# Four lines instead of five for VectorE's exponentials, with one of them on GpSimd: a gated attention kernel on one core

## The chip, the cores and the metric

The kernel runs on one core of one Trainium2 chip. The metric is the device time of one execution in microseconds. The core has TensorE (PE in the profile, its weight loads PEld), VectorE (DVE), ScalarE (ACT), GpSimd (POOL) and SyncE (SP, which here issues DMAs).

## What is computed

One input of 2048 tokens by 512 features goes through two attention branches, which are mixed by a gate. Cut to what matters:

```python
H, Dh = 32, 16                                   # both branches: 32 heads of 16
# branch A: softmax attention over all 2048 keys
q, k, v = split(x @ A_wqkv)
p = softmax(einsum("bhqd,bhkd->bhqk", q, k) * Dh ** -0.5)
a = einsum("bhqk,bhkd->bhqd", p, v) @ A_wo
# branch B: linear attention with feature maps
phi = lambda t: concat(softmax(t @ w_phi), softmax(-(t @ w_phi)))
kv, z = einsum(phi(k), v), phi(k).sum(tokens)
b = (phi(q) @ kv / (phi(q) @ z + 1e-6)) @ B_wo
g = sigmoid((x * gate_w).sum(-1, keepdims=True))
out = g * a + (1 - g) * b
```

Weights, input and output are bf16. Branch A has 32 x 2048 x 2048 = 134 million exponentials, and these fill the time.

## The kernel before

**Tiles.** A unit is one tile of scores: 128 keys by 512 queries of one head. A pack is four units, of four heads. There are 4 chunks of queries, 8 groups of four heads and 16 blocks of keys, so 512 packs and 2048 units. The scores of up to four heads are computed beside each other in the rows of TensorE's array (`_scores`), into PSUM. The exponentials of a pack are multiplied with the values of its four heads beside each other in the columns (`_values`), and add up in one PSUM bank; a column of ones in the values gives the softmax's denominator. So an approximate exponential needs no maximum, and a factor that all of a row's terms share would cancel.

**Two ways to an exponential.** Most units go to ScalarE: `_exp` takes groups of three and two units from a ring of five PSUM banks (`NRING`, `GROUPS`), and writes bf16 into `ET`. The packs that `SHARES` names (so many of the 16 packs of each group of heads) go to VectorE in `_vector_batch`. There four instructions named `v_bits` move the four score tiles from PSUM to a block of 128x2048 fp16, scaled. Then five instructions named `v_line` each add a constant of `LINES` to the block, cut it off at zero and write the result as int16 into another block: the bits, read as bf16, are a piecewise linear exponential. The five differ by a shift, and their sum is closer to the exponential than one is. TensorE multiplies each of the five with the values (`pvx`), so that the sum is made in PSUM. The blocks are a ring of `NBLK` buffers; the last line of a pack overwrites its input block.

**Other work of VectorE.** It evicts all projections from PSUM, normalizes branch A (`_normed`: `n_t1`, `n_den`, `n_rec`, `n_mul`, `n_back`) and makes the softmax of branch B's feature maps (`_b_part`, the names with `b_`). GpSimd fills constants at the start and does nothing after that. TensorE also runs products with a zero operand (`_fill`) that add nothing to the result.

**Order.** Nothing is ordered by loops. Each operation is given to a planner (`Plan.op`) with a cost, a priority and what it reads and writes. `Plan.order` simulates the engines with these costs and fixes one order of instructions for each engine, `Plan._waits` derives the semaphores from the dependencies, and `emit` writes the program. The tables `HURRY`, `EASE`, `QEASE`, `LEASE`, `OEASE` and `NUDGE` shift priorities of single operations. Each engine runs its list in order, so an instruction that waits holds up all that is behind it on its engine.

Of the kernel before, what the change touches and what calls it, by code (L numbers as in the profile page):

```python
# [7 lines left out]
ALU = mybir.AluOpType  # L8
AX = mybir.AxisListType

P = 128
# [9 lines left out]
LINES = (15902.272, 15921.612, 15944.747, 15969.563, 16002.022)  # L21
# [22 lines left out]
class Op:  # L44
    def __init__(self, eng, fn, cost, name, prio, rel, kind, lat, groups=None):
# [6 lines left out]
        self.need = False  # L52
        self.acquire = None
# [15 lines left out]
class Plan:  # L69
# [11 lines left out]
    LATE = 9.5  # L81

# [73 lines left out]
    def order(self):  # L156
# [9 lines left out]
        pe = (None, (0.0,) * 4, 0.0)  # L166
        recent = []
# [5 lines left out]
        while left:  # L173
            best = None
            for e in self.ENGS:
                found, limit = [], 1e9
                for o in avail[e]:
# [83 lines left out]
            else:  # L261
# [3 lines left out]
                free[e] = o.end  # L265
            queues[e].append(o)
            left -= 1
# [103 lines left out]
class _Kernel:  # L371
# [5 lines left out]
    NBLK, LEAD = 7, 4  # L377
# [7 lines left out]
    OREL = 5  # L385
    ENDS = 10
    HURRY = (2.9, 1.9, -1.8, 7.6, -1.0, -4.5, 21.3, 1.1, 0.8, 0.0, 8.8, 2.1, 8.3, -5.2, 0.0, 0.0, 1.3, -3.6, 0.0, 0.0, 0.0,
# [4 lines left out]
    QEASE = (0, 0.0, 13.2, 0.0, 5.2, -10.0, 15.5, 0.2, 0.0, 5.8, -9.4, -3.4, 2.9, 7.9, 0.0, 3.2)  # L392
    LEASE = (0.4, 3.6, -6.9, 0.7, -0.7, -0.7, -13.7, 20.2, -4.9, 11.4)
    OEASE = (14.9, 0.6, -1.3, 18.1, 9.6, 11.8, 25, 9.7, 0.8, -5.2, 1.0, 3.6, 6.4, 0, 0, 0)
    EASE = (0.0, 1.2, 0.4, 8.9, 0.0, 0.0, 2.6, 0.0, 0.0, -3.6, 11.9, 0.0, 3.7, 1.9, -4.9, -1.5, 11.8, 2.3, 2.1, 0.0, 0.3, -0.9,
# [4 lines left out]
    NUDGE = {  # L400
        'b_even': {10: 1.3},
        'b_grid': {7: 15.3, 8: 16.2},
        'b_max': {1: -22.3, 3: 17.1, 13: 1.8, 18: -26.3, 20: -8.7, 22: -4.2, 24: 8.3, 31: 2.8, 37: 25.7, 50: -15.5,
            52: -17.0, 57: -15.0, 58: -4.1, 59: -17.8, 60: 8.7, 61: 3.5, 75: 18.1},
        'b_mul': {7: -11.9},
        'b_octave': {1: 2.1, 2: 5.8},
        'b_out': {14: 13.9},
        'b_part': {1: 12.9},
        'b_slope': {8: -4.1},
        'b_square': {3: -9.2, 4: 3.0, 10: -10.4},  # L410
        'b_sum': {20: -16.6},
        'b_top': {4: 5.4, 18: 11.1},
        'bv': {1: 3.4, 5: 7.0, 7: -2.3, 8: 23.3, 13: -5.3, 14: -18.8, 28: 7.4, 29: -3.5, 42: 7.7},
        'den': {20: 18.4, 26: 10.5},
        'kproj': {1: -5.8, 13: -7.7, 21: 5.1, 24: 5.0, 29: 9.7, 33: 4.1, 36: -11.3, 45: 10.9, 53: -3.2, 61: 4.4, 64: 14.2},
        'kproj_ev': {11: -6.1},
        'n_back': {3: 5.6, 14: -6.3},
        'n_den': {4: -7.0, 11: 10.1, 18: -4.3},
        'n_rec': {9: 30.0},
        'n_t1': {7: 5.1, 11: -15.8, 18: 3.7, 21: -10.4},  # L420
        'num': {6: 16.9},
        'out_ev': {4: -7.4, 11: -21.6},
        'outa': {14: -2.6, 22: -6.7, 27: -11.9, 35: -14.0, 36: 4.1, 37: 6.8, 56: 1.4, 57: -11.0},
        'pq': {6: 18.3, 13: -4.0, 20: 7.4, 25: -11.0, 33: 30.0, 42: 26.3, 53: -4.4, 57: -6.4, 61: 6.2, 65: -2.7, 81: 2.9,
            85: 2.4, 87: 9.1, 95: 6.2, 113: -12.4, 115: -7.9, 117: -12.5, 128: 11.3},
        'pq_ev': {16: 5.7},
        'pvx': {4: 12.2, 6: 5.5, 7: 24.2, 9: -2.8, 10: -10.3, 14: -16.0, 16: -24.7, 17: -6.4, 18: -3.2, 19: 1.7, 33: -3.7,
# [3 lines left out]
        'qproj_ev': {11: -19.0, 14: -6.7, 18: 9.1, 19: -2.2},  # L431
        'v_bits': {58: 19.2, 215: 15.2},
        'v_line': {1: 20.1, 4: 6.9, 9: -10.7, 28: 14.5, 30: -9.2, 32: 9.9, 33: 16.5, 40: -13.6, 44: 7.7, 68: -9.4, 71: -16.6,
# [7 lines left out]
        'vproj': {23: 23.6, 26: 4.1, 28: 9.2, 41: 3.1, 49: 3.9, 51: -7.7, 60: 18.9, 61: 3.2},  # L441
        'vqk': {4: 11.2, 6: -19.7, 9: 15.9, 14: 10.3, 19: 8.4, 22: 13.9, 26: -23.0, 28: -5.9, 33: -28.9, 35: -2.8, 46: -14.6,
# [36 lines left out]
    def _memory(self, ctx):  # L479
# [1153 lines left out]
```

## Time and profile before

| | |
|---|---|
| median of 3 runs | 788.67 us (788.64 to 789.07) |
| the profiled execution's time | 788.6 us |
| its span in the trace | 786.6 us |
| granted TensorE clock | 1.0 |
| exponentials on ScalarE | 683 instructions for 1708 units |
| packs on VectorE | 85, with 340 `v_bits` and 425 `v_line` |
| instructions of GpSimd | 15, the last at 27.59 us |

In the profile a busy time is the time in which an engine has at least one instruction running, and a mean is that of single instructions. Instructions that follow each other on ScalarE or VectorE overlap by some tenths or hundredths of a microsecond, so the busy time of a group, divided by its count, is closer to what one of them costs than the mean is. A group's row ends with the idle time just before its instructions and what ended it.

### The profile page before, as it was taken

The page shows a single profiled execution, that of the slowest core. Times are in us where ns is not written, and L with a number is a line of the kernel's source. Part 1 is how long each engine was busy: PE and PEld are TensorE (multiplying, and loading weights), DVE is VectorE, ACT ScalarE, POOL GpSimd, SP SyncE. Part 2 cuts the span into 40 slices and gives each one's busy share as a digit, 9 for nine tenths or more (in the row PEclk, how much of TensorE's full clock was granted, in tenths as well). Part 3 has the DMA queues.
Part 4 walks back from the last instruction along what each step waited for, and adds up shares of the span by engine and source line. Part 5 has one row for each costly group of instructions (what it writes and reads, how often), then busy time and mean ns, then how long its engine had stood idle before and what let it go on. Part 6 is the DMA issues. An engine that isn't in the chain of part 4 may idle for free.

```text
span 786.6 us, 20365 instructions
## 1 busy us (share of the span) xinstructions
PE 768.9 (98%) x9024; PEld 262.6 (33%) x9024; DVE 767.8 (98%) x1340; ACT 775.5 (99%) x688; POOL 8.3 (1%) x15
## 2 busy tenths in 40 slices
PE   8999999999999999999999999999999999999998
PEld 4333333333232322333332223323333322233345
DVE  5999999999999999999999999999999999999997
ACT  7999999999999999999999999999999999999997
POOL 3000000000000000000000000000000000000000
PEclk9999999999999999999999999999999999999999
DMA  9600000000000000210000004102101000031000
GB/s 239 192 8 2 8 3 6 1 2 8 8 2 2 1 8 9 55 29 8 1 9 2 8 22 63 35 1 45 30 17 28 9 2 21 8 76 21 2 2 30
DMA packets 49031, 20.06 MB, mean 26 GB/s; under 512 B 38704, under 2 KB 48944, under 8 KB 48944
## 3 DMA queue, kind: packets, MB, share of 16 engines
q1 hardware_dynamic: 48272, 18.58, 10.2%
q8 instruction: 70, 1.15, 0.6%
q10 hardware_dynamic: 672, 0.20, 0.1%
q14 instruction: 17, 0.14, 0.1%
HBM read 6.31 MB, written 2.10 MB: 11 GB/s over the span
## 4 chain that ended last, share of the span: by engine, by line
ACT 91%; DVE 6%; PE 3%; issue 0%
ACT ET L1075 91%; DVE blocks L942 1%; DVE blocks L931 1%; PE ps L1024 1%; DVE WB L1282 1%; PE ps L744 1%; PE ps L696 0%; PE ps L840 0%; PE ps L1147 0%; PE ps L1571 0%; DVE kT L766 0%; DVE V L846 0%; DVE xT L727 0%; PE ps L715 0%; DVE T L1200 0%
## 5 line engine op out<-in xcount | busy, mean ns | idle before, releaser
L1075 ACT ACTIVATE ET<-ps 128x1536 bf16<-128x1536 f32 (+1 forms) x683 | 773.2, 1332 | 1.0 <-PE ps L1024 0.7
L1024 PE MATMUL ps<-qT,kT 32*128 32x512 bf16 (+2 forms) x2248 | 303.4, 364 | 9.5 <-ACT ET L1075 5.4
L942 DVE TENSOR_SCALAR blocks<-blocks 128x2048 int16<-128x2048 f16 x317 | 209.5, 682 | 0.6 <-PE ps L1147 0.4
L931 DVE TENSOR_SCALAR blocks<-ps 128x512 f16<-128x512 f32 x292 | 191.4, 680 | 2.4 <-PE ps L1024 2.1
L1024 PEld LDWEIGHTS ps<-qT,kT 32*128 32x128 bf16 x2248 | 83.2, 91 | 261.0 <-ACT ET L1075 151.4
L1147 PE MATMUL ps<-ET,V 128*32 128x512 bf16 (+2 forms) x1872 | 158.0, 364 | 0.6 <-DVE V L846 0.3
L1156 PE MATMUL ps<-kT,zero 128*32 128x512 bf16 x1820 | 150.3, 384 | 0.0
L1147 PE MATMUL ps<-blocks,V 128*32 128x512 bf16 (+1 forms) x1616 | 133.6, 363 | 1.1 <-DVE blocks L942 0.6
L1147 PEld LDWEIGHTS ps<-ET,V 128*32 128x32 bf16 x1872 | 45.0, 96 | 53.5 <-issue 33.3
L1156 PEld LDWEIGHTS ps<-kT,zero 128*32 128x32 bf16 x1820 | 38.0, 94 | 64.6 <-issue 55.0
L1147 PEld LDWEIGHTS ps<-blocks,V 128*32 128x32 bf16 x1616 | 38.5, 95 | 52.4 <-DVE blocks L942 22.1
L744 PE MATMUL ps<-WB,xT 128*128 128x512 bf16 x192 | 53.8, 382 | 0.8 <-DVE blocks L931 0.6
L744 PE MATMUL ps<-xT,WA 128*128 128x512 bf16 (+1 forms) x124 | 35.3, 379 | 1.1 <-DVE xT L727 0.6
L942 DVE TENSOR_SCALAR blockz<-blocks 128x2048 int16<-128x2048 f16 x48 | 32.6, 679 | 0.0
L942 DVE TENSOR_SCALAR blocks<-blockz 128x2048 int16<-128x2048 f16 x48 | 32.0, 683 | 0.1
L931 DVE TENSOR_SCALAR blockz<-ps 128x512 f16<-128x512 f32 x48 | 31.7, 679 | 0.2 <-PE ps L1024 0.2
L1200 DVE STREAM_TRANSPOSE T<-ps 128x512 f32<-128x512 f32 (+1 forms) x35 | 23.2, 663 | 2.2 <-PE ps L1147 1.9
L1147 PE MATMUL ps<-blockz,V 128*32 128x512 bf16 (+1 forms) x264 | 23.5, 363 | 0.0
L744 PEld LDWEIGHTS ps<-WB,xT 128*128 128x128 bf16 x192 | 14.5, 97 | 24.7 <-issue 9.7
L1309 DVE TENSOR_SCALAR bq<-ps 128x512 bf16<-128x512 f32 x32 | 21.4, 674 | 0.2
L840 PE MATMUL ps<-WA,xT 128*128 128x128 bf16 x256 | 19.9, 220 | 0.2 <-DVE blocks L931 0.2
L1361 DVE TENSOR_TENSOR octs<-octs,brec 128x4096 bf16<-128x4096 bf16 (+1 forms) x10 | 18.6, 1858 | 0.0
(104 smaller groups left out, 434.3 us busy)
## 6 DMA issues: line engine op xcount, KB each, us to landing
qT<-qraw SPq DMA_DIRECT2D x120, 16.0 KB, 1.8
xn<-in_A_x_dram SPq DMA_DIRECT2D x3, 512.0 KB, 6.1
WB<-in_B_wqkv_dram SPq DMA_DIRECT2D x3, 512.0 KB, 5.3
out_dram<-WB SPq DMA_DIRECT2D x12, 128.0 KB, 1.7
WA<-in_A_wqkv_dram SPq DMA_DIRECT2D x3, 384.0 KB, 4.5
xn<-in_A_x_dram SPq DMA_DIRECT2D x2, 256.0 KB, 3.6
WoA<-in_A_wo_dram SPq DMA_DIRECT2D x1, 512.0 KB, 6.0
WoB<-in_B_wo_dram SPq DMA_DIRECT2D x1, 512.0 KB, 6.8
```

The lines of the kernel that those rows point to most:

```text
L744: mm = op("PE", lambda e, c=c: e.matmul(self._bank(job)[:, 0:n], lhs(c), rhs(c), start=(c == 0), stop=(c == 3)), self.c_pe(n), reads=reads ...
L840: ins = e.matmul(self._bank(job)[:, P * tt:P * tt + P], self.xT[:, 4 * j + tt, c], self.WA[:, 2, c, P * cp:P * cp + P], start=(c == 0), st ...
L931: parts.append(op("DVE", lambda e, j=j, job=job: e.tensor_scalar(x[:, j, :], self._bank(job), SCALE * LOG2E * 128, None, op0=ALU.mult), se ...
L942: op("DVE", lambda e, tile=tile, line=line: e.tensor_scalar(tile.rearrange("p n q -> p (n q)").bitcast(I16), x.rearrange("p n q -> p (n q) ...
L1024: ins = e.matmul(out[u][:, cols], self.kT[32 * i:32 * i + 32, cp, kt * TOK:(kt + 1) * TOK], self.qT[32 * i:32 * i + 32, s, q], start=True, ...
L1075: o = plan.op("ACT", lambda e: e.activation(self.ET[:, a % NS:a % NS + n, :], self.ps[:, a % NR:a % NR + n, :], ACT.Exp, scale=SCALE), sel ...
L1147: ins = e.matmul(self._bank(ot)[32 * i:32 * i + 32, to], self.V[:, kt, g8 // 2, v0:v0 + 32], tile[:, cols], start=first and j == 0, stop=o ...
L1156: ins = e.matmul(self._bank(ot)[32 * i:32 * i + 32, lo:QCH], self.zero[:], self.kT[:, 0, lo:QCH], start=False, stop=False, tile_position=( ...
L1200: return e.transpose(to, acc if alone else acc.rearrange("p (e b d) -> p e b d", e=2, b=8))
L1282: done.append(op("DVE", lambda e, c=c, job=job: e.tensor_copy(self.WB[:, s, c].rearrange("p (g f i) -> p g f i", g=8, i=4), self._bank(job ...
L1309: [lambda e, b, k=k: e.tensor_scalar(bq[:, k].rearrange("p (g s v) -> p g s v", g=8, s=2)[:, :, 0, :], b.rearrange("p (g v) -> p g v", g=8 ...
L1361: dve("b_octave", two(n), lambda e: e.tensor_tensor(grid.rearrange("p (a s f i) -> p a s f i", s=2, f=DH, i=4), up.rearrange("p a (f i) -> ...
```

## The change

The five lines become four, in two pairs: two are multiplied with the values, two with a copy of the values that is scaled by 0.69921875 (`WEIGHT`). The copy `VW` is made on GpSimd by `_weighted`: 64 instructions named `v_scale`, four for each group of 32 packs. In 63 of the packs the first line is computed by GpSimd instead of VectorE (`POOLED`). `SHARES` now names 92 packs instead of 85, so ScalarE has 1680 units. The ring of blocks has 6 buffers instead of 7.

GpSimd and VectorE share access to SBUF for some kinds of instructions. The planner now has a list of names (`PORT`), and no such operation of one engine is ordered beside one of the other: an operation on the list gets a dependency on the other engine's latest listed one, which becomes a semaphore wait. The VectorE instructions that read PSUM (`v_bits`, projections, `n_t1`) are not on the list. The tables of priorities are new throughout, and two release points (`OREL`, `SCALED`) were set.

```diff
-LINES = (15902.272, 15921.612, 15944.747, 15969.563, 16002.022)
+LINES = ((15976.573, 0), (16041.341, 1), (16008.864, 0), (16073.128, 1))
+WEIGHT = 0.69921875
...
+        self.port = name in Plan.PORT
...
+    PORT = {"v_line", "v_scale", "gate_z", "gate_h", "gate_b", "n_den", "n_mul", "kvbd", "b_grid", "b_rest", "b_max", "b_top",
+            "b_octave", "b_square", "b_slope", "b_even", "b_odd", "b_part", "b_out", "b_sum", "b_ratio", "b_mul"}
+    GUARD, GIVE, TAKE, REST = 0.0, 0.1, 0.12, 0.1
...
+            pool = [(max(free["POOL"], o.dep_t, port["DVE"].end + self.GIVE if port["DVE"] else 0.0), o) for o in avail["POOL"]
+                    if o.port and o.rel <= self.now]
+            booked = min(pool, key=lambda x: x[0]) if pool else None
...
+                    if o.port and e == "POOL" and port["DVE"]:
+                        t = max(t, port["DVE"].end + self.GIVE)
+                    elif o.port and e == "DVE":
+                        if port["POOL"]:
+                            t = max(t, port["POOL"].end + self.TAKE)
+                        if booked and t > booked[0] - self.GUARD:
+                            t = max(t, booked[0] + booked[1].cost + self.TAKE)
...
+            if o.port and e in port:
+                other = port["DVE" if e == "POOL" else "POOL"]
+                if other is not None:
+                    o.deps.append(other)
+                port[e] = o
...
-    NBLK, LEAD = 7, 4
+    NBLK, LEAD = 6, 4
+    POOLED = (1, 1, 0, 1, 0, 0, 1, 1, 1, 1, 1, 1, 0, 1, 0, 0, 1, 1, 1, 1, 1, 1, 1, 1, 1, 0, 0, 0, 1, 0, 1, 1, 0, 1, 1, 1, 1, 1,
...
+    SCALED, POOL = 10, 0.00084
...
-    OREL = 5
+    OREL = 2
...
+        self.VW = sb("VW", [P, 4, 4 * 136 + 16], BF16)
...
-    SHARES = (1, 2, 1, 1, 2, 3, 2, 2, 1, 3, 3, 2, 2, 4, 4, 5, 2, 4, 1, 2, 3, 2, 5, 4, 3, 4, 0, 4, 2, 6, 2, 3)
+    SHARES = (0, 2, 1, 3, 3, 0, 3, 2, 4, 3, 2, 4, 3, 5, 3, 3, 4, 1, 4, 3, 3, 3, 2, 6, 3, 2, 5, 3, 3, 3, 3, 3)
...
+    def _weighted(self, n):
+
+        cp = n % 4
+        for q in range(4):
+            self.plan.op("POOL", lambda e, q=q: e.tensor_scalar(
+                self.VW[:, q, 0:544].rearrange("p (t v) -> p t v", v=136), self.V[:, 4 * q:4 * q + 4, cp, 0:136], WEIGHT, None,
+                op0=ALU.mult), 0.165 + 544 * self.POOL, reads=[self.b_V[cp][q]], writes=[self.b_VW[q]], name="v_scale",
+                prio=32 * n - self.SCALED + 4 * q, rel=32 * n - 16 + 4 * q, deps=[self.o_wpad])
...
-        for k, line in enumerate(LINES):
+        for k, (line, weighted) in enumerate(LINES):
...
+            pooled = k == 0 and self.POOLED[number]
+            op("POOL" if pooled else "DVE", lambda e, tile=tile, line=line: e.tensor_scalar(
+                flat(tile).bitcast(I16), flat(x), line, 0.0, op0=ALU.add, op1=ALU.max),
+                0.165 + 4 * QCH * self.POOL if pooled else 0.066 + 4 * QCH * 0.000262,
+                reads=[b_x], writes=[b_to], name="v_line", prio=prio)
...
+            values = self.b_VW[quarter] if weighted else self.b_V[cp][quarter]
...
+                v = 136 * (kt % 4) + v0
+                values = self.VW[:, kt // 4, v:v + 32] if weighted else self.V[:, kt, g8 // 2, v0:v0 + 32]
```

More of the change, by code (lines that the diff above doesn't have):

```diff
@@ L166, in order @@
         pe = (None, (0.0,) * 4, 0.0)
+        port = {"DVE": None, "POOL": None}
         recent = []
@@ L264, in order @@
                     self._land(o)
-                free[e] = o.end
+                free[e] = o.end + self.REST * (e == "POOL" and o.port)
             queues[e].append(o)
+            if o.port and e in port:
[3 more added lines that the diff above has]
+                port[e] = o
             left -= 1
@@ L384 @@
     VREL0 = 5
-    OREL = 5
+    OREL = 2
     ENDS = 10
-    HURRY = (2.9, 1.9, -1.8, 7.6, -1.0, -4.5, 21.3, 1.1, 0.8, 0.0, 8.8, 2.1, 8.3, -5.2, 0.0, 0.0, 1.3, -3.6, 0.0, 0.0, 0.0,
[4 rows of a table removed]
[L392 to L395, printed above, removed]
[4 rows of a table removed]
@@ L630, in _consts @@
         self.o_vpad = op("POOL", lambda e: e.memset(self.V[:, :, :, 136:], 0.0), 0.5, prio=-69)
+        self.o_wpad = op("POOL", lambda e: e.memset(self.VW[:, :, 544:], 0.0), 0.2, prio=-68)
         self.o_vbones = op("POOL", lambda e: e.memset(self.VB[:, :, :, 64:65], 1.0), 0.3, prio=-20)
@@ L907, in _plan_vector @@
                 lambda k=k, p=p, due=due: self._vector_batch(k, p, due))
+        for n in range(4 * self.NQC):
+            self.hooks.setdefault(32 * n, []).append(lambda n=n: self._weighted(n))
         for due, fn in self.linear:
@@ L934, in _vector_batch @@
         b_x.writers, b_x.readers = parts, []
-        g8 = p // self.NT % 8
-        block = self._block(p)
-        values = self.b_V[g8 // 2][p % self.NT // 4 if block is None else kt].writers
+        cp = p // self.NT % 8 // 2
+        quarter = p % self.NT // 4 if self._block(p) is None else kt
         ot = self.ot[a]
-        for k, line in enumerate(LINES):
+        flat = lambda t: t.rearrange("p n q -> p (n q)")
+        for k, (line, weighted) in enumerate(LINES):
             to = ks[(k + 1) % len(ks)]
             b_to, tile = self.b_blocks[to], self._block_at(to)
-            op("DVE", lambda e, tile=tile, line=line: e.tensor_scalar(
-                tile.rearrange("p n q -> p (n q)").bitcast(I16), x.rearrange("p n q -> p (n q)"), line, 0.0,
-                op0=ALU.add, op1=ALU.max), 0.066 + 4 * QCH * 0.000262, reads=[b_x], writes=[b_to], name="v_line", prio=prio)
+            pooled = k == 0 and self.POOLED[number]
[3 more added lines that the diff above has]
+                reads=[b_x], writes=[b_to], name="v_line", prio=prio)
             src = {i: tile[:, i, :].bitcast(BF16) for i in range(4)}
-            o = op("PE", None, self._wide(4 * p), deps=[self.opened[a], *values], reads=[b_to], name="pvx",
+            values = self.b_VW[quarter] if weighted else self.b_V[cp][quarter]
+            o = op("PE", None, self._wide(4 * p), deps=[self.opened[a]], reads=[b_to, values], name="pvx",
                    prio=p + 2.6, kind="col", array=0.0533 * 4, groups=(0, 1, 2, 3))
-            o.fn = lambda e, o=o, src=src: self._values(e, ot, p, src, o)
+            o.fn = lambda e, o=o, src=src, w=weighted: self._values(e, ot, p, src, o, w)
             o.strips = (ot, (0, 1, 2, 3))
@@ L966, in _attention @@
         self.b_octs, self.b_part, self.b_blocks = Buf(), Buf(), [Buf() for _ in range(self.NBLK)]
+        self.b_VW = [Buf() for _ in range(4)]
         for b in (self.b_octs, self.b_part, self.b_blocks[-1]):
@@ L1138, in _pv, with _values @@
             self.late = []
-    def _values(self, e, ot, p, src, op):
+    def _values(self, e, ot, p, src, op, weighted=0):
         g8 = p // self.NT % 8
@@ L1146, in _values @@
                 v0 = 17 * (2 * i + g8 % 2)
-                ins = e.matmul(self._bank(ot)[32 * i:32 * i + 32, to], self.V[:, kt, g8 // 2, v0:v0 + 32], tile[:, cols],
+                v = 136 * (kt % 4) + v0
+                values = self.VW[:, kt // 4, v:v + 32] if weighted else self.V[:, kt, g8 // 2, v0:v0 + 32]
+                ins = e.matmul(self._bank(ot)[32 * i:32 * i + 32, to], values, tile[:, cols],
                                start=first and j == 0, stop=ot.final[i] is op and j == len(parts) - 1,
```

78 lines of the change are left out of this document (46 added, 32 removed), and 45 rows, old and new, of tables (EASE, HURRY, NUDGE, POOLED).

## The prediction

> **What bounds the kernel now.** I read the page's shares first, then the chain of work that ended last, then the groups by line, then the stretches of time, and last the timeline of single instructions. The page and its chain:
>
> ```profile
> span 786.6 us, 20365 instructions
> PE 768.9 (98%) x9024; PEld 262.6 (33%) x9024; DVE 767.8 (98%) x1340; ACT 775.5 (99%) x688; POOL 8.3 (1%) x15
> ...
> ACT 91%; DVE 6%; PE 3%; issue 0%
> ```
>
> Three engines look full, so the shares do not separate them; the chain does: 91% of it is ScalarE. The groups and stretches say why:
>
> ```profile
> L1075 ACT ACTIVATE ET<-ps 128x1536 bf16<-128x1536 f32 (+1 forms) x683 | 773.2, 1332 | 1.0 <-PE ps L1024 0.7
> ```
> ```profile
> 300.00:400.00 100.00, 98.11 (x1214) 31.42 (x1206) 99.90 (x166) 100.00 (x90) 0.00 (x0) 1.00 0.10 21
> 400.00:500.00 100.00, 98.83 (x1114) 31.42 (x1111) 99.89 (x169) 99.84 (x89) 0.00 (x0) 1.00 0.12 22
> ```
> ```profile
> PEld ps L1024 <- ACT ET L1075: 151.4, 385, 0.8
> ```
>
> The columns of a stretch are PE, PEld, DVE, ACT, POOL. ScalarE's 683 exponentials run back to back: 773.2 / 683 = 1.132 us each, 1.0 us idle in all. TensorE is the least bound of the three: it waited 151.4 us for ScalarE to free score banks. VectorE is a close second: 99.9 of 100 us in mid-run. So a change pays by exactly what it takes from ScalarE, and only while VectorE keeps up. What lies outside each engine's work: the span less the exponentials is 786.6 - 773.2 = 13.4 us, and less VectorE's busy time 786.6 - 767.8 = 18.8 us (head, tail and a few waits).
>
> **ScalarE's part of the change.** A pack is four score tiles; a pack given to VectorE leaves ScalarE. The shares add up to 85 packs before and 92 after, so 28 tiles leave ScalarE, and the changed program holds 672 exponentials where 683 stood: 11 x 1.132 = 12.5 us off the chain. If ScalarE stays full, the span is 786.6 - 12.5 = 774.1 us.
>
> **VectorE's part.** Its rows, and its pace when nothing is awaited:
>
> ```profile
> L942 DVE TENSOR_SCALAR blocks<-blocks 128x2048 int16<-128x2048 f16 x317 | 209.5, 682 | 0.6 <-PE ps L1147 0.4
> L931 DVE TENSOR_SCALAR blocks<-ps 128x512 f16<-128x512 f32 x292 | 191.4, 680 | 2.4 <-PE ps L1024 2.1
> ```
> ```profile
> 402.13 0.69 DVE L942 TENSOR_SCALAR blockz<-blocks 128x2048 int16<-128x2048 f16 x1
> ...
> 402.95 0.10 PEld L1147 LDWEIGHTS ps<-blocks,V 128*32 128x32 bf16 x4 [0.23 <-DVE blockz L942]
> ...
> 406.41 1.28 DVE L931 TENSOR_SCALAR blocks<-ps 128x512 f16<-128x512 f32 x2
> ...
> 410.02 2.50 DVE L942 TENSOR_SCALAR blocks<-blocks 128x2048 int16<-128x2048 f16 x4
> ```
>
> Durations overlap: four lines take 2.50 us where four times 0.682 would be 2.73, so one line costs (2.50 - 0.68) / 3 = 0.607 us, and two evictions of scores (L931) take 1.28, so 0.60 each. The next instruction starts 0.08 us before the last one's end.
>
> - Lines on VectorE: 85 x 5 = 425 before; 92 x 4 = 368 less 63 sent to GpSimd = 305 after. 120 x 0.607 = 72.8 us go.
> - Evictions: 7 x 4 = 28 more, 28 x 0.60 = 16.8 us come.
> - Busy time: 767.8 - 72.8 + 16.8 = 711.8 us.
>
> **GpSimd's part, which no row shows.** The trace has nothing like a two-step scalar operation over 128x2048 on GpSimd. The nearest rows:
>
> ```profile
> L634 POOL MEMSET qT<- 128x2048 bf16 x1 | 1.8, 1806 | 0.0
> L637 POOL TENSOR_TENSOR wphi<-wphin,heads 128x512 bf16<-128x512 bf16 x1 | 1.1, 1053 | 1.7 <-DMA wphin<-in_B_w_phi_dram 1.7
> L854 POOL MEMSET gwb<- 128x544 bf16 x1 | 0.6, 632 | 0.0
> ```
>
> The fill of the same 2048 elements writes only: 1.81 us, a lower end. The product of two tensors takes 1053 ns for 512, four times that is 4.21 us: an upper end, because the line reads one tensor and not two. I take 1.9 us, close to the fill, with reading beside writing and 0.1 us to start. A weighted copy of values (544 elements) is 0.6 us by the fill of 544, up to 1.12 us by the product. GpSimd is then busy 63 x 1.9 + 64 x 0.6 = 158 us, a fifth of the span, so it has time; the question is what it does to VectorE.
>
> The change makes every VectorE instruction marked as port user wait for the GpSimd port user before it, and the other way. Queued behind such a wait on VectorE is all that follows, evictions of score banks too; TensorE waits for those banks and ScalarE for TensorE. What VectorE may do meanwhile is unmarked work: evictions from PSUM above all. I took the order of the changed program's instructions and, for each group of GpSimd operations, counted the VectorE instructions between the one that GpSimd waits for and the first that waits for GpSimd, nearly all of them evictions at 0.6 us. Needed from the end of VectorE's instruction: the hand-off to GpSimd (0.13 us, as from VectorE to TensorE above: the line that starts at 402.13 ends at 402.82, and its reader starts at 402.95), the operation, the hand-off back, and the 0.08 us overlap. For the hand-off back there is one row, of the start:
>
> ```profile
> 1.18 0.29 POOL L618 TENSOR_SCALAR_AFFINE_SELECT iden<-iden 128x128 bf16<-128x128 bf16 x1 [0.18 <-POOL zero L633]
> ```
> ```profile
> 1.50 0.35 DVE L622 TENSOR_REDUCE mask<-iden 128x1 f32<-128x64 bf16 x2 [1.50 <-POOL iden L618]
> ```
>
> GpSimd's end at 1.47 to VectorE's start at 1.50 is 0.03 us; I take 0.1, between this and 0.13. A line alone needs 0.13 + 1.9 + 0.1 + 0.08 = 2.21 us, a copy alone 0.91 us. The counted cover:
> - 41 waits for a line alone: 3 have 0.6 us of cover, 4 have 1.2, 19 have 1.8, 15 have 2.4 or more. Short by 3 x 1.6 + 4 x 1.0 + 19 x 0.4 = 16 us.
> - 28 waits for copies alone: 8 have 0.6, the others 1.2 or more. Short by 3 us.
> - 20 waits for a line and one or two copies (2.8 us or more): 1 has 1.2, 5 have 1.8, 5 have 2.4, 9 have 3.0 or more. Short by 9 us.
>
> Together 28 us; ten other waits are for something long done. The same count gives 24 us with a line of 1.81, 43 with 2.2, 56 with 2.4, 96 with 3.0 and 183 with 4.21 (copies in proportion).
>
> VectorE's bound is 711.8 + 28 + 18.8 = 758.6 us, under ScalarE's 774.1 by 15 us; before, the same sum gave the span itself. Cut into sixteen equal shares of the exponentials (47.6 us each), VectorE's work with its stalls is 41 to 52 us in each, 46.4 in the mean, and the one heaviest share lies between two light ones. Where nothing changes hands VectorE is thus freer than before.
>
> The Trainium skill (SBUF — State Buffer, "Who interferes with whom") says that GpSimd's port pair is VectorE's second pair, locked for a whole instruction by a VectorE operation in a two-port mode or with two SBUF inputs, and that an operation with at most one SBUF input outside those modes is not held. By that rule the evictions that I counted as cover run freely, which the sum above assumes; no row here shows GpSimd beside VectorE's steady work.
>
> **What has one answer.** TensorE loses 57 groups of four products (425 groups to 368) and some of its fillers, and has 151.4 us of waiting to give: nothing on the chain. The ring of blocks shrinks from 7 to 6 while a pack takes 4 instead of 5, so 1.5 packs are in flight where 1.4 were. Copies of values are put 16 packs ahead of their use; if one is late, TensorE's queue stands, and ScalarE with it after the banks it has. The new priorities only reorder; the before kernel shows 1.0 us of ScalarE idle from such order, and stalls of VectorE in lumps of up to 1.6 us may add some: I allow 0.4 us, and up to 7 us in the range. The tail after the last exponential is kept (its earlier release may move it by 1 us either way).
>
> **The sum.** 786.6 - 12.5 + 0.4 = 774.5 us of span. The profiled execution's time was 788.6 us, 2.0 above its span and 0.1 under the median 788.67 of the runs, so no correction: 774.5 + 2.0 = 776.5 us. Its own range is 773 to 784.
>
> **The rivals.**
> - *GpSimd's line is slow (slower).* A line that costs 3.0 us, halfway between the two rows, makes VectorE the bound: 711.8 + 96 + 18.8 + 2.0 = 829 us. It decides from the point where the stalls reach 56 us, at 2.4 us a line: there the gain of VectorE is used up and the time is the old one. At 2.7 us it is 808, at 4.21 us 916. For it: the product's 2.06 ns an element, and that the line converts two types and does two steps. Against it: the fill's 0.88 ns an element. Chance 0.16. The Trainium skill (GPSIMD Engine Reference, "Performance versus the Vector engine") gives a best case of about 1.8 cycles an element for a tight loop, but 1.03 for bodies of at most two operations; by the first a line is 3.07 us, an estimate from that page, and the time near this rival's, by the second 1.76 us. The trace's fill and product bracket both and do not choose.
> - *GpSimd's work costs a little more (2.1 to 2.5 us a line), or its queue stands.* Of the 64 copies 28 wait for TensorE to have read the old ones, and a line behind such a copy waits with it, and VectorE with that. VectorE then becomes the bound by itself at 2.2 us (stalls 43 us), and the time is 776 to 795, centre 786. Chance 0.14, of which half faster, 0.03 the same, 0.04 slower.
> - *The two engines hold each other off in all work, not just in what is marked.* Then every operation of GpSimd stands in VectorE's time: 63 x 2.13 + 64 x 0.83 = 187 us, and 711.8 + 187 + 18.8 + 2.0 = 920 us. No row speaks for or against it, as GpSimd's last instruction of before comes early:
>
> ```profile
> 27.59 0.49 POOL L855 COPY gwb<-gw 128x16 bf16<-128x16 bf16 x1 [17.40 <-DMA gw<-in_gate_w_dram]
> ```
>
> Chance 0.06.
>
> That the change doesn't reach ScalarE is no rival: the order of the program already has 672 exponentials.
>
> **How the numbers follow.** The forecast has 0.64, the rivals 0.16, 0.14 and 0.06. A measurement of this kernel tells a change from none at about 0.2%, 1.6 us. Faster: 0.64 + 0.07 = 0.71; same 0.03; slower 0.16 + 0.04 + 0.06 = 0.26. The slow line and the full exclusion hold 0.22, so the range has to reach a little into the first of them: to 808 us, a line of 2.7 us, which leaves out some 0.18. Below, 773 us is the forecast with a tail and hand-offs at their best.
>
> **What would show it.** Right: 672 exponentials at 1.13 us with a few us idle at most, ScalarE still nine tenths of the chain, VectorE's busy time near 712 us with some 28 us of waits for GpSimd, lines on GpSimd at 1.8 to 2.0 us. Wrong: lines above 2.4 us, VectorE's waits for GpSimd above 50 us and ScalarE idle in the rows of its exponentials; or evictions (L931's successor) longer than 0.68 us while GpSimd runs.

## The result, and the profile after

The changed kernel takes 1176.17 us (median of 4 runs, 1175.13 to 1177.69), the kernel before 788.69 us beside it (788.64 to 789.07): 1.4913 times as long, with a 95% interval of 1.4887 to 1.4939. The forecast was 776.5 us with a range of 773 to 808. It missed by 400 us, and on the other side.

The profiled execution took 1177.69 us. The page of the changed kernel, its span, shares, clock and chain, and the costliest groups (in a row: busy us and mean ns of one, then the idle time just before and what ended most of it):

```profile
span 1175.8 us, 19708 instructions
PE 891.5 (76%) x8643; PEld 269.7 (23%) x8688; DVE 735.1 (63%) x1248; ACT 787.6 (67%) x677; POOL 554.4 (47%) x143
...
PEclk9899897988877697876887767788977777787888
...
POOL 41%; DVE 28%; PE 27%; issue 2%; ACT 1%; POOLq 1%; DVEq 0%
...
L1125 ACT ACTIVATE ET<-ps 128x1536 bf16<-128x1536 f32 (+1 forms) x672 | 785.3, 1250 | 378.7 <-PE ps L1074 376.8
L989 POOL TENSOR_SCALAR blocks<-blocks 128x2048 int16<-128x2048 f16 x38 | 269.3, 7086 | 243.5 <-DVE blocks L989 91.9
...
L977 DVE TENSOR_SCALAR blocks<-ps 128x512 f16<-128x512 f32 x368 | 242.7, 684 | 84.4 <-PE ps L1074 82.9
L989 DVE TENSOR_SCALAR blocks<-blocks 128x2048 int16<-128x2048 f16 x269 | 181.7, 686 | 155.1 <-POOL VW L954 54.9
L989 POOL TENSOR_SCALAR blockz<-blocks 128x2048 int16<-128x2048 f16 x25 | 177.1, 7086 | 155.6 <-DVE blocks L989 70.4
L954 POOL TENSOR_SCALAR VW<-V 128x544 bf16<-128x544 bf16 x64 | 100.6, 1575 | 206.2 <-PE ps L1199 70.5
```

Read the chain first. ScalarE had 91% of it and has 1%; GpSimd has 41%, then VectorE and TensorE. No engine is full any more (TensorE 76%, VectorE 63%, ScalarE 67%, GpSimd 47%), so the time is not one engine's work but work that waits in turn. The rows of GpSimd say for what: a line takes 7086 ns where 1.9 us was forecast, a weighted copy 1575 ns where 0.6 us was. The exponentials are the 672 that were expected, and 378.7 us of idle time stand before them, where before it was 1.0. The same stretches of mid-run as before (PE, PEld, VectorE, ScalarE, GpSimd, granted clock):

```profile
300.00:400.00 100.00, 73.02 (x703) 18.74 (x701) 57.05 (x87) 61.91 (x53) 57.20 (x12) 0.79 0.01 2
400.00:500.00 100.00, 78.20 (x723) 19.82 (x722) 63.74 (x103) 68.09 (x58) 43.36 (x11) 0.81 0.01 4
```

VectorE's 99.9 of 100 us became 57 and 64. The waits show how one engine's wait becomes the next one's (engine and line, what it waited for: us in all, how often, the longest):

```profile
ACT ET L1125 <- PE ps L1074: 376.8, 191, 6.7
...
PE ps L1199 <- POOL blocks L989: 101.5, 27, 5.4
...
DVE blocks L977 <- PE ps L1074: 82.9, 102, 4.4
...
PE ps L1199 <- POOL blockz L989: 73.1, 18, 5.5
...
DVE blocks L989 <- POOL VW L954: 54.9, 18, 7.2
DVE blocks L989 <- POOL blockz L989: 49.3, 11, 6.6
...
DVE blocks L989 <- POOL blocks L989: 39.0, 9, 5.1
```

One case of it, from the timeline of all engines (start, duration, idle time before in brackets):

```profile
507.93 0.68 DVE L977 TENSOR_SCALAR blocks<-ps 128x512 f16<-128x512 f32 x1
508.10 7.08 POOL L989 TENSOR_SCALAR blockz<-blocks 128x2048 int16<-128x2048 f16 x1 [8.05 <-DVE bsum L1438]
...
508.53 0.94 DVE L1448 RECIPROCAL brec<-bsum 128x128 f16<-128x128 f32 x1
...
509.39 0.63 DVE L977 TENSOR_SCALAR blocks<-ps 128x512 f16<-128x512 f32 x1
...
515.14 1.58 POOL L954 TENSOR_SCALAR VW<-V 128x544 bf16<-128x544 bf16 x1
515.23 0.11 PEld L1199 LDWEIGHTS ps<-blockz,V 128*32 128x32 bf16 x4 [5.22 <-POOL blockz L989]
...
516.44 1.45 ACT L1125 ACTIVATE ET<-ps 128x1536 bf16<-128x1536 f32 x1 [5.10 <-PE ps L1074]
516.82 0.29 DVE L1456 TENSOR_TENSOR brec<-bsum,brec 128x128 f16<-128x128 f32 x1 [6.81 <-POOL VW L954]
```

VectorE has two evictions and a reciprocal as cover for a line and a copy of GpSimd, and ends them at 510.02. Then it stands 6.81 us, until GpSimd has done both. TensorE's next weight load, which reads that line, stands 5.22 us; behind it in TensorE's queue are the scores, so ScalarE stands 5.10 us. All three engines are idle together, behind one instruction of GpSimd.

### The profile page after: what moved, and what is told of

The parts are those of the page before. It is cut to its first block, busy times and chain, and to the rows that moved or that the text cites. A ratio compares the mean times of both kernels' runs of the same rounds, so it can differ in the third digit from the quotient of the medians.

```text
span 1175.8 us, 19708 instructions
## 1 busy us (share of the span) xinstructions
PE 891.5 (76%) x8643; PEld 269.7 (23%) x8688; DVE 735.1 (63%) x1248; ACT 787.6 (67%) x677; POOL 554.4 (47%) x143
## 4 chain that ended last, share of the span: by engine, by line
POOL 41%; DVE 28%; PE 27%; issue 2%; ACT 1%; POOLq 1%; DVEq 0%
POOL blocks L989 23%; POOL blockz L989 14%; PE ps L1199 9%; PE ps L1074 9%; DVE blocks L989 8%; DVE blocks L977 6%; POOL VW L954 4%; PE ps L1208 4%; PE ps L779 2%; ACT ET L1125 1%; DVE blockz L989 1%; DVE octs L1413 1%; DVE bq L1407 1%; DVE bq L1428 1%; PE ps L875 1%
## 5 line engine op out<-in xcount | busy, mean ns | idle before, releaser
L1125 ACT ACTIVATE ET<-ps 128x1536 bf16<-128x1536 f32 (+1 forms) x672 | 785.3, 1250 | 378.7 <-PE ps L1074 376.8
L989 POOL TENSOR_SCALAR blocks<-blocks 128x2048 int16<-128x2048 f16 x38 | 269.3, 7086 | 243.5 <-DVE blocks L989 91.9
L1074 PE MATMUL ps<-qT,kT 32*128 32x512 bf16 (+2 forms) x2248 | 348.2, 417 | 34.3 <-DVE blocks L977 11.7
L977 DVE TENSOR_SCALAR blocks<-ps 128x512 f16<-128x512 f32 x368 | 242.7, 684 | 84.4 <-PE ps L1074 82.9
L989 DVE TENSOR_SCALAR blocks<-blocks 128x2048 int16<-128x2048 f16 x269 | 181.7, 686 | 155.1 <-POOL VW L954 54.9
L989 POOL TENSOR_SCALAR blockz<-blocks 128x2048 int16<-128x2048 f16 x25 | 177.1, 7086 | 155.6 <-DVE blocks L989 70.4
L954 POOL TENSOR_SCALAR VW<-V 128x544 bf16<-128x544 bf16 x64 | 100.6, 1575 | 206.2 <-PE ps L1199 70.5
L1199 PE MATMUL ps<-ET,V 128*32 128x512 bf16 (+2 forms) x1844 | 181.8, 425 | 6.1 <-DVE blocks L977 5.8
L1208 PE MATMUL ps<-kT,zero 128*32 128x512 bf16 (+1 forms) x1776 | 176.1, 458 | 0.0
L1199 PE MATMUL ps<-blocks,V 128*32 128x512 bf16 (+1 forms) x540 | 59.7, 456 | 104.7 <-POOL blocks L989 101.5
L1199 PE MATMUL ps<-blocks,VW 128*32 128x512 bf16 (+1 forms) x808 | 84.0, 429 | 25.2 <-DVE blocks L989 24.6
L1199 PE MATMUL ps<-blockz,V 128*32 128x512 bf16 (+1 forms) x268 | 30.1, 457 | 73.8 <-POOL blockz L989 73.1
```

The lines of the kernel that those rows point to most:

```text
L954: self.plan.op("POOL", lambda e, q=q: e.tensor_scalar(self.VW[:, q, 0:544].rearrange("p (t v) -> p t v", v=136), self.V[:, 4 * q:4 * q + 4 ...
L977: parts.append(op("DVE", lambda e, j=j, job=job: e.tensor_scalar(x[:, j, :], self._bank(job), SCALE * LOG2E * 128, None, op0=ALU.mult), se ...
L989: op("POOL" if pooled else "DVE", lambda e, tile=tile, line=line: e.tensor_scalar(flat(tile).bitcast(I16), flat(x), line, 0.0, op0=ALU.add ...
L1074: ins = e.matmul(out[u][:, cols], self.kT[32 * i:32 * i + 32, cp, kt * TOK:(kt + 1) * TOK], self.qT[32 * i:32 * i + 32, s, q], start=True, ...
L1125: o = plan.op("ACT", lambda e: e.activation(self.ET[:, a % NS:a % NS + n, :], self.ps[:, a % NR:a % NR + n, :], ACT.Exp, scale=SCALE), sel ...
L1199: ins = e.matmul(self._bank(ot)[32 * i:32 * i + 32, to], values, tile[:, cols], start=first and j == 0, stop=ot.final[i] is op and j == le ...
```

## The experiments

The runs ask four things: what a scalar operation costs on GpSimd, whether its length alone makes the loss, what the waits for the shared access do, and what the change is worth without GpSimd.

**m1_forms: the forms by themselves.** This kernel does none of the reference's work. GpSimd runs each form alone, three times; then VectorE starts four instructions of a kind behind a GpSimd line. The forms, cut short:

```python
e.tensor_scalar(oi[:], h[:], 100.0, 0.0, op0=ALU.add, op1=ALU.max)   # fp16 to int16, two steps; also 1024, 512 wide
e.tensor_scalar(oi[:], h[:], 100.0, None, op0=ALU.add)               # one step
...                                                                  # fp16 to fp16, bf16 to bf16, fp32 to fp32
e.tensor_scalar(ob[:, 0:544], hb[:, 0:544], 0.7, None, op0=ALU.mult)
e.tensor_copy(oi[:], h[:]); e.tensor_tensor(oh[:], h[:], h2[:], ALU.add); e.memset(oh[:], 1.0)
```

> A kernel of its own, without the reference's work: GpSimd runs forms of one-input scalar operations over 128x2048 one by one, three times each, on an otherwise idle core, then nine times the line beside four VectorE instructions (three times four lines of fp16, three times four evictions from PSUM, three times four products of two bf16 tensors). Theory T, that types and conversion make the line slow: fp32 to fp32 with two steps takes about 1.9 us, as the prediction had it, fp16 to int16 7.1 us. Theory K, that two steps make it slow: one step takes under 3.6 us in any type, two steps 7 us in any type. Theory R, that a scalar operation on GpSimd has this rate: all forms within 30% of 7.1 us. For the second part: if ports are locked, lines and products of VectorE last until the line of GpSimd ends, some 7 us, and evictions keep 0.60 us each.

The groups of GpSimd by form (L87, L82 and L99 have two steps, L85, L81 and L86 one; L99 is the line that VectorE's instructions stand behind):

```profile
L99 POOL TENSOR_SCALAR oi<-h 128x2048 int16<-128x2048 f16 x9 | 63.7, 7079 | 1.0 <-POOL tock L97 0.3
...
L87 POOL TENSOR_SCALAR of<-f 128x2048 f32<-128x2048 f32 x3 | 21.3, 7089 | 0.2
L82 POOL TENSOR_SCALAR oh<-h 128x2048 f16<-128x2048 f16 x3 | 21.3, 7084 | 0.2
...
L85 POOL TENSOR_SCALAR ob<-hb 128x2048 bf16<-128x2048 bf16 x3 | 16.1, 5374 | 0.2
L81 POOL TENSOR_SCALAR oi<-h 128x2048 int16<-128x2048 f16 x3 | 16.1, 5372 | 0.2
...
L94 POOL TENSOR_TENSOR oh<-h 128x2048 f16<-128x2048 f16 x3 | 12.1, 4046 | 0.3
...
L92 POOL CAST oi<-h 128x2048 int16<-128x2048 f16 x3 | 5.7, 1897 | 0.2
...
L95 POOL MEMSET oh<- 128x2048 f16 x3 | 5.4, 1805 | 0.2
L86 POOL TENSOR_SCALAR ob<-hb 128x544 bf16<-128x544 bf16 x3 | 4.7, 1569 | 0.2
```

An addition of two tensors takes 4.05 us and a scalar operation with one input tensor 5.37, or 7.08 with two steps: fewer inputs do not make it cheaper. The types do nothing: fp32 to fp32, fp16 to fp16 and fp16 to int16 lie within 10 ns of each other, which rules out that the conversion makes the line dear. The second step adds 1.7 us, but one step is already nearly three times the conversion alone (1.90 us). So the theory that all scalar forms lie near 7.1 us comes nearest, and the one that a single step would be under 3.6 us fell. The 1024 and 512 wide lines took 3.63 and 1.92 us, 3.37 ns an element and some 0.2 us to start.

The timeline of both engines, for four lines and for four evictions of VectorE behind a GpSimd line:

```profile
274.01 7.08 POOL L99 TENSOR_SCALAR oi<-h 128x2048 int16<-128x2048 f16 x1
...
274.64 8.79 DVE L57 TENSOR_SCALAR do<-dh 128x2048 int16<-128x2048 f16 x4
...
303.82 7.08 POOL L99 TENSOR_SCALAR oi<-h 128x2048 int16<-128x2048 f16 x1
...
304.45 2.47 DVE L59 TENSOR_SCALAR dp<-ps 128x512 f16<-128x512 f32 x4
```

The four lines, 2.50 us without GpSimd, take 8.79: GpSimd ends at 281.09, and 2.34 us later they are done. The four evictions take 2.47 us, as if alone. Four products of two tensors, the third kind, end 1.9 us after GpSimd does. So the chip itself holds VectorE's line back for a whole GpSimd instruction, and leaves its reads of PSUM alone. That agrees with the rule that the prediction weighed (the Trainium skill, SBUF — State Buffer, "Who interferes with whom").

**e6_quarter and e7_half: the same kernel with shorter GpSimd work.** The order of instructions and all waits stay; GpSimd computes only a quarter or a half of each of its lines and weighted copies, and the rest of those tiles keeps what it held (one block is filled once at the start for that, and one line is left whole).

```diff
+            cut = 512 if pooled and number != 1 else 4 * QCH          # e7: 1024
-                flat(tile).bitcast(I16), flat(x), line, 0.0, op0=ALU.add, op1=ALU.max),
+                flat(tile).bitcast(I16)[:, 0:cut], flat(x)[:, 0:cut], line, 0.0, op0=ALU.add, op1=ALU.max),
...
-                self.VW[:, q, 0:544]..., self.V[:, 4 * q:4 * q + 4, cp, 0:136], WEIGHT, None,
+                self.VW[:, q, 0:136]..., self.V[:, 4 * q:4 * q + 1, cp, 0:136], WEIGHT, None,     # e7: 272, two
```

> The order of instructions and every wait are those of the changed kernel, but GpSimd's lines write only 512 of their 2048 elements and its copies of values 136 of 544 (the rest of the work is left out; the first line into one buffer stays whole, and a fill of one block is added at the start). Theory A, that only the size of GpSimd's work was wrong in the prediction: at 3.46 ns an element a line is 1.8 us, near the 1.9 us of the prediction, the stalls of VectorE count up to 15 to 20 us, ScalarE is full again, the granted clock 1.0, and the time is 776 to 783 us. Theory B, that the hand-offs and the new order cost by themselves whatever the line's length: it stays above 900 us.

> As the quarter, with 1024 of 2048 elements in a line and 272 of 544 in a copy. Theory A: a line of 3.5 us, stalls of VectorE by the prediction's count 117 to 125 us, so 711.8 + 120 + 18.8 + 2 = 853 us, and by the excess that the whole line showed over the same count (1176 against 1111, a sixth of the stalls) up to 875. Theory B: near the changed kernel's 1176 us, over 1000.

A quarter: 779.06 us (777.16 to 781.36), 0.9883 of before (0.9859 to 0.9908). A half: 888.12 us (886.83 to 889.41), 1.1262 (1.124 to 1.1285). First the page of the quarter, then that of the half:

```profile
ACT 74%; PE 13%; DVE 11%; DMA 1%; POOL 0%; issue 0%; SPq 0%
...
L1128 ACT ACTIVATE ET<-ps 128x1536 bf16<-128x1536 f32 (+1 forms) x672 | 761.6, 1315 | 3.6 <-PE ps L1077 3.5
```
```profile
L1128 ACT ACTIVATE ET<-ps 128x1536 bf16<-128x1536 f32 (+1 forms) x672 | 775.9, 1257 | 99.9 <-PE ps L1077 97.5
...
L991 POOL TENSOR_SCALAR blocks<-blocks 128x1024 int16<-128x1024 f16 x38 | 138.1, 3633 | 239.7 <-DVE blocks L991 92.7
```

With lines of 1.93 us, the length that the prediction had assumed, ScalarE has the chain again, is idle for 3.6 us, and the time is within 2.6 us of the forecast. With 3.63 us it is idle for 99.9. The two differ in nothing but the length of GpSimd's instructions, so the length is what costs, and it turns between these two. The quarter lies in its expectation; the half came 35 us above the centre of its expectation and 13 above its upper end: the count of covered time gives too little once waits are long.

**e4_no_port_waits: no waits between the two engines' port users.** The order, the work and all data dependencies stay.

```diff
             if o.port and e in port:
                 other = port["DVE" if e == "POOL" else "POOL"]
-                if other is not None:
-                    o.deps.append(other)
                 port[e] = o
```

> The same order of instructions, without the semaphore waits that keep marked work of GpSimd and VectorE apart; all waits for data stay, and all work is done. Theory A, that the chip itself locks the two out of each other (the Trainium skill, SBUF - State Buffer, says so): a marked VectorE instruction that meets a running line is held for its rest, so the time stays within 10% of 1176 us, 1060 to 1250. Theory C, that the waits are what costs and the ports would share: VectorE runs beside the lines, GpSimd is busy 63 x 7.1 + 64 x 1.6 = 548 us beside it, and the time falls below 950 us.

1242.05 us (1241.35 to 1242.75), 1.575 of before (1.5719 to 1.5782): 66 us more than with the waits. VectorE's lines in its groups by form:

```profile
L987 DVE TENSOR_SCALAR blocks<-blocks 128x2048 int16<-128x2048 f16 x269 | 422.5, 1581 | 16.9 <-PE ps L1197 8.5 <-POOL blocks L987 7.8
...
L975 DVE TENSOR_SCALAR blocks<-ps 128x512 f16<-128x512 f32 x368 | 243.0, 682 | 95.2 <-PE ps L1072 93.1
...
L987 DVE TENSOR_SCALAR blockz<-blocks 128x2048 int16<-128x2048 f16 x36 | 73.5, 2041 | 0.2 <-PE ps L1197 0.2
```

That is in the expected range, near its top. The idle time went into the instructions: 269 lines take 1581 ns in the mean where they took 686, while the evictions keep 682. So the semaphore waits are not the loss: without them the chip makes VectorE wait all the same. What the waits save is shown as a sum only; why the bare lock is 66 us dearer was not separated. The lock holds GpSimd too: in this run its lines take 7.38 us in the mean and its weighted copies 1.80, for 7.09 and 1.58 with the waits, 33 us of busy time more.

**e9_all_as_copies and e10_lines_as_copies: the same width with a cheap operation.** GpSimd copies instead of adding and cutting off, over the full tiles. e9 replaces lines and weighted copies, and so leaves out the first line's constant and cut-off in 63 packs, and the weight; e10 replaces the lines alone.

```diff
-            op("POOL" if pooled else "DVE", lambda e, tile=tile, line=line: e.tensor_scalar(
+            op("POOL" if pooled else "DVE", lambda e, tile=tile, line=line, pooled=pooled: e.tensor_copy(
+                flat(tile), flat(x)) if pooled else e.tensor_scalar(
...
-            self.plan.op("POOL", lambda e, q=q: e.tensor_scalar(self.VW..., self.V..., WEIGHT, None, op0=ALU.mult)    # e9 only
+            self.plan.op("POOL", lambda e, q=q: e.tensor_copy(self.VW..., self.V...)
```

> The changed kernel's order and all of its waits, and GpSimd touches all 2048 and 544 elements, but with a plain copy in place of its scalar operations (the add and the clipping of its lines and the weight of its copies of values are left out). Theory A, that the prediction failed in nothing but the price of a GpSimd instruction: a copy of 2048 was 1.89 us in the measurement of forms, so the line has the prediction's own price of 1.9 us and the copy of values about 0.55 us; stalls by the prediction's count are 21 to 27 us, and the time is its 776.5 us, 774 to 781. Rival B, that 63 lines of full width cost VectorE or TensorE something beside their duration (bytes through the shared port, later blocks): above 800 us.

> As the one before, but the 64 weighted copies of values are real (a product with the weight, 1.58 us each); only the lines are plain copies. It splits the loss between the 63 lines and the 64 weighted copies. By the prediction's count the stalls are 55 to 63 us, so VectorE is the bound: 711.8 + 59 + 18.8 + 2 = 792 us, 783 to 800. If the weighted copies were a main cause of the changed kernel's loss, it would be far above: their 64 x 1.58 = 101 us all on the path give 870 us.

e9: 780.13 us (780.03 to 783.09), 0.9902 of before (0.9881 to 0.9922). e10: 810.19 us (808.17 to 812.21), 1.0271 (1.024 to 1.0301). The pages of e9 and of e10:

```profile
L1125 ACT ACTIVATE ET<-ps 128x1536 bf16<-128x1536 f32 (+1 forms) x672 | 762.4, 1310 | 4.5 <-PE ps L1074 4.0
...
L988 POOL COPY blocks<-blocks 128x2048 f16<-128x2048 f16 x38 | 71.9, 1893 | 241.6 <-DVE blocks L989 89.1
L954 POOL COPY VW<-V 128x544 bf16<-128x544 bf16 x64 | 40.8, 640 | 202.4 <-PE ps L1199 60.7
```
```profile
L954 POOL TENSOR_SCALAR VW<-V 128x544 bf16<-128x544 bf16 x64 | 100.2, 1568 | 196.5 <-PE ps L1200 56.2
```

Copies over full tiles at 1.89 and 0.64 us, nearly the prices of the prediction, give the time of the prediction within 3.6 us. So neither the width, nor the tiles, nor the waits are the cause, only what an instruction costs. e9 is where it was expected. Taken in this order, the step from e9 to e10, 30 us, is the dear weighted copies, and the step from e10 to the changed kernel, 366 us, is the dear lines. e10 came 10 us above the upper end of its expectation, though VectorE's waits for GpSimd sum to 38 us only, where 55 to 63 were counted: VectorE also waits for TensorE for 40 us (13 before), and is busy for 722.7 us where the count has 711.8.

**e2_no_gpsimd and e11_no_gpsimd_retimed: the change without GpSimd.** All lines and weighted copies go to VectorE. e2 keeps the changed kernel's priorities and 92 packs; e11 has 87 packs, with priorities and two of the planner's constants (`LEAD`, `OREL`) searched anew for that order.

```diff
-            pooled = k == 0 and self.POOLED[number]
+            pooled = False
...
-            self.plan.op("POOL", lambda e, q=q: e.tensor_scalar(
+            self.plan.op("DVE", lambda e, q=q: e.tensor_scalar(      # cost 0.066 + 544 * 0.000262
```

> All four lines and the weighted copies of values on VectorE, nothing on GpSimd in mid-run; 92 packs, two weights and 6 blocks as in the changed kernel, all work done; the priorities are the changed kernel's, which were set for another arrangement. Theory A, that GpSimd's instructions are the whole loss: VectorE's busy time is 711.8 + 63 x 0.607 + 64 x 0.2 = 763 us and the time 784 us by its bound, with up to 40 us more for priorities that no longer fit: 780 to 825 us, clock 1.0. Theory D, that other parts of the change (6 blocks, weights, 92 packs) cost too: above 850 us.

> As the kernel without GpSimd in mid-run (four lines, two weights, the weighted copies of values on VectorE, all work done), with 87 packs and priorities searched anew for this arrangement. Theory A, that the change without GpSimd is sound and 818.6 us came from priorities that did not fit: two packs more than before leave ScalarE, 8 / 2.5 x 1.132 = 3.6 us, so 785 us; VectorE's busy time is 767.8 - 77 x 0.607 + 8 x 0.60 + 18 = 744 us and not the bound. 782 to 790. Theory D, that 6 blocks or the weights cost by themselves: above 795.

e2: 818.61 us (818.3 to 818.91), 1.0377 of before (1.0357 to 1.0398). e11: 790.73 us (788.14 to 795.18), 1.003 (1.0016 to 1.0045). The page of e2, then that of e11:

```profile
L1125 ACT ACTIVATE ET<-ps 128x1536 bf16<-128x1536 f32 (+1 forms) x672 | 762.7, 1318 | 40.9 <-PE ps L1199 25.4
...
L954 DVE TENSOR_SCALAR VW<-V 128x544 bf16<-128x544 bf16 x64 | 18.3, 289 | 1.9 <-PE ps L1199 1.6
```
```profile
PE 753.1 (95%) x8557; PEld 256.0 (32%) x8604; DVE 746.7 (94%) x1335; ACT 773.7 (98%) x685; POOL 8.1 (1%) x16
...
L1125 ACT ACTIVATE ET<-ps 128x1536 bf16<-128x1536 f32 (+1 forms) x680 | 771.4, 1323 | 9.7 <-PE ps L1074 9.5
```

One of e11's idle stretches of ScalarE, and a stretch soon after it (columns as in the stretches of mid-run above; the granted clock is the third number from the end):

```profile
586.30:596.50 10.20, 9.73 (x68) 2.21 (x65) 7.11 (x12) 7.07 (x6) 0.00 (x0) 0.50 0.01 2
600.00:612.00 12.00, 11.60 (x125) 3.75 (x123) 11.63 (x23) 12.00 (x12) 0.00 (x0) 1.00 0.18 45
```

A weighted copy takes 289 ns on VectorE, and 1575 on GpSimd. Merely taking GpSimd out wins back 358 us, so it is the detour over GpSimd and not the four lines that costs. But the four lines alone then gain nothing. VectorE's work in e11 came as expected (746.7 us for 744), and with 87 packs 680 exponentials are left on ScalarE; but in the profiled execution (794.94 us, among the longest of its 12) ScalarE was idle for 9.7 us before late scores, a term that the expectation did not have. The trace shows where: in four stretches of mid-run, 23.8 us together, the granted clock was a half, and 8.5 us of that idle time lie in them or within 2 us behind them. The median just misses the expected range, and the 12 times order by the mean granted clock, from 788.14 us at 0.993 to 795.18 at 0.985. What lowers the clock there no run shows.

**e12_first_line_free: another place for the first line.** The queries are scaled by `SCALE * LOG2E * 128` when they are projected. Then a score needs no factor in `v_bits`, and its two steps are free for the first line's constant and cut-off; it writes that line's int16 at once. The other three lines add differences of constants to it. All else is as in e11, with 93 packs, and with priorities and `LEAD` searched for this order. All of the computation is done. (Adding a difference after the cut-off leaves those terms that were cut off at the difference of two lines' constants instead of at zero: as bits, a bf16 of next to nothing.)

```diff
-                x[:, j, :], self._bank(job), SCALE * LOG2E * 128, None, op0=ALU.mult), self.c_dve(512),
+                x[:, j, :].bitcast(I16), self._bank(job), LINES[0][0], 0.0, op0=ALU.add, op1=ALU.max), self.c_dve(512),
...
+            if k:
+                op("DVE", lambda e, tile=tile, line=line: e.tensor_scalar(
+                    flat(tile).bitcast(I16), flat(x).bitcast(I16), line - LINES[0][0], 0.0, op0=ALU.add, op1=ALU.max),
...
-            self.ET[...], self.ps[...], ACT.Exp, scale=SCALE),
+            self.ET[...], self.ps[...], ACT.Exp, scale=1 / UP),          # UP = LOG2E * 128
```

> As that kernel, with the first of the four lines made by the eviction itself: the queries are scaled when they are projected, so that the eviction from PSUM adds the first line's constant, clips at zero and writes int16, and the other three lines add a difference to that. All work is done. 93 packs, priorities searched for it. Theory A, that a line removed is worth more than a line moved: 32 tiles leave ScalarE, 32 / 2.5 x 1.132 = 14.5 us, so 774 us, 771 to 780; VectorE's busy time is 767.8 - 146 x 0.607 + 32 x 0.60 + 18 = 716 us. Theory D: above 790.

774.73 us (774.44 to 775.67), 0.9825 of before (0.9813 to 0.9838): faster than both kernels. The page of e12:

```profile
PE 737.5 (95%) x8452; PEld 251.9 (33%) x8496; DVE 719.6 (93%) x1290; ACT 762.0 (99%) x676; POOL 8.1 (1%) x16
...
L1124 ACT ACTIVATE ET<-ps 128x1536 bf16<-128x1536 f32 (+1 forms) x671 | 759.7, 1309 | 0.8 <-PE ps L1073 0.7
...
L978 DVE TENSOR_SCALAR blocks<-ps 128x512 int16<-128x512 f32 x372 | 240.9, 680 | 12.7 <-PE ps L1073 12.0
```

The eviction takes 680 ns with two steps and an int16 result, as it did with one step and fp16. So a line has gone at no price, VectorE is at 719.6 us (716 was expected), and ScalarE, idle for 0.8 us, bounds the kernel with 671 exponentials. This is what the change was forecast to bring, without GpSimd.

## Why the prediction was wrong

**The step that failed is the price of GpSimd's line.** The prediction set the product of two tensors, 4.21 us, as the "upper end, because the line reads one tensor and not two". No row bore that reason out, and m1_forms refutes it: one input and two steps take 7.08 us, an addition of two tensors 4.05. Both rows that the price lay between were operations of other kinds, and the true value lies outside them by 68%. The weighted copy failed by the same step: 1.58 us, over the "up to 1.12". e9, which only puts the price back, brings the time back: 780.13 for 776.5.

Neither of the two figures cited beside rival 1 fits this operation either (the Trainium skill, GPSIMD Engine Reference, "Performance versus the Vector engine"): by the first a line would take 3.07 us, by the second 1.76, both estimates from that page, and 7.09 are measured. That page's section "Engine selection" says that one-input operations run at roughly line rate. Here no one rate holds for them: a copy takes 0.92 ns an element, a scalar operation 2.6 with one step and 3.5 with two.

The changed kernel's planner holds the same price (`POOL`: 0.165 + 2048 x 0.00084 = 1.89 us), so its order was made for such lines. No run has an order made for lines of 7.09 us; how much of the loss that would win back stays open.

**The mechanism was rival 1's, and its size was cut off by the same step.** That rival makes VectorE the bound by its stalls, from 2.4 us a line on, and e6 and e7 lie on the two sides of that, at 1.93 and 3.63 us. The rival's times ended at 916 us only because its lines ended at 4.21. Its own count with 7.09 and 1.58 us gives stalls of 379 us and 711.8 + 379 + 18.8 + 2.0 = 1112 us. With the right price the prediction would have been slower by 41%, not faster.

**66 us are left that the count doesn't give**, from 1112 to the profiled 1177.7. Summed over the trace, VectorE is idle for 302 us until GpSimd is done and for 133 us until TensorE is, beside 735.1 us busy. So it waits less for GpSimd than counted, and far more for TensorE. The waits shown above have the reason that the prediction denied with "nothing on the chain": TensorE works in order and stands 101.5 + 73.1 us before products of GpSimd's lines, and the scores that VectorE evicts as cover stand behind them (82.9 us of waits before `v_bits`, where it was 2.1). Another part is VectorE's busy time, 735.1 for 711.8: 9 us of these 23 are there without the long waits too (720.8 in e9), and the others may come from instructions that start after a wait and so don't overlap the one before.

A further part can be the granted clock (0.82 in this run, 1.0 before). The trace has it at a half for 425 us of the span. ScalarE is busy for 43% of these and for 81% of the rest. In e11, where VectorE waits for GpSimd nowhere in mid-run, ScalarE was idle for 7.1 of the 23.8 us at half clock; the same share of 425 us would be 127 us, an estimate, and more than the 66. So the clock can be all that the count lacks, and some of the stalls with it. With the order and the waits kept, it goes with the length of GpSimd's instructions: 0.998 in e6, 0.96 in e7, 0.82 here. No run holds the stalls and changes the clock.

**What held.**
- 672 exponentials, and 12.5 us off ScalarE where GpSimd is cheap: 762.4 us busy in e9, where 773.2 less 12.5 is 760.7. Of e9's 3.6 us above the forecast, some 3 are ScalarE's idle time (4.5 for 1.4).
- Evictions as free cover: in the trace of after, the 145 that ran wholly beside a GpSimd instruction took 684 ns, the other 223 also 684. Rival 3, exclusion in all work, is thus refuted.
- Lines do hold each other off, with or without the semaphores (m1_forms, e4).
- The hand-offs were priced high: from VectorE's end to GpSimd's start 0.084 us in the median, back 0.033, for 0.13 and 0.1. With these the counted stalls are 370 us instead of 379, so they do not matter.

Rival 2, a little more cost or a queue that stands, comes nearest to e10, though there the copies are dear and not the lines: lines at 1.89 us and copies at 1.57 give 810 us, above the 795 where it ended. The dearer copies alone were enough to lose the gain.

## What to carry to other kernels

An operation that the trace doesn't show is not bounded by rows of other operations: an end of a range needs a reason that some row bears out, and "fewer inputs" was none. Before work moves to an engine that has done nothing, time that very form alone, in the width it will have. Where two engines hold each other off, compare a single instruction's length with the work that can run beside it, not the sums: GpSimd was busy for under half of the span, and it took the whole kernel down because one line (7.1 us) is longer than what VectorE has at hand (in most waits 1.8 to 2.4 us by the prediction's count). And look first for a free second step in an instruction that runs anyway: e12's eviction made the line at no cost.

## What the hardware showed

- On GpSimd a scalar operation over 128x2048 takes 5.37 us with one step and 7.08 with two, whatever the types tried; an addition of two tensors takes 4.05, a copy or a conversion 1.89 and a fill 1.80. So the kind of operation sets the price there, and for a scalar operation the number of steps.
- On VectorE an eviction from PSUM takes 680 ns with one step or two, to fp16 or int16.
- Without semaphores the lock shows inside the durations: lines of VectorE in e4 take 1581 and 2041 ns in the mean for 686, with no wait in the profile to name. A mean duration that grows while the shape stays is thus a wait too.
